# Attention and gated MLP on one core: in the first batch, the turn of u for column 1 is queued ahead of the score transposes, and the gating of a column is fixed ahead of the next squares on VectorE

## The chip, the cores and the metric

The kernel runs on one core of one Trainium2 chip. The metric is the device time of one execution in microseconds (us). The kernel before, run 11 times on one chip, gave 1217.6 to 1223.4 us.

Every ratio below is the record's ratio of a kernel's fast runs to those of the kernel before in the same rounds; it is not quite the ratio of the medians that stand beside it, nor exactly that of the plain means (u1_early: 1.0014 by means, 1.0008 on record). A 95% interval follows in brackets.

## The reference

Eight batches of attention with squared-ReLU scores and a gate `u`, then an MLP with a cosine activation over all 24064 tokens. It is cut to what matters:

```python
# u, v: [8, 3008, 256]   z: [8, 3008, 64]
scores = (1.0 / S) * np.matmul(z, z.transpose(0, 2, 1))
attn = np.maximum(scores, 0.0) ** 2
x = u * np.matmul(attn, v)              # the gating
h = x @ w_in                            # 256 -> 2048
out = (h * np.cos(h)) @ w_out           # 2048 -> 256
```

## The kernel before

A batch is worked off in six columns `c` of 512 tokens. For each block of scores, TensorE (PE) makes the scores, ScalarE (ACT) or VectorE (DVE) takes the ReLU, and DVE squares the result into a slot `s`. There are 18 slots for all score blocks. The output of a column is gated by `u`, which must stand transposed in SBUF. Two kinds of transposes are issued by SyncE (SP), in one fixed order: the turn of u (`ut<-ust`, 256 KB) and the score transposes (`s<-s`, 512 KB each), which spare PE the other half of the symmetric scores.

```python
def load(dst, src):                      # loads are issued by GpSimd, in order
    hold(nc.gpsimd.dma_start(dst, src))  # hold: wait until PE has come this far

def turn_u(b, c):
    ut = utpool.tile([P, NDH, CW], FP16, name="ut")
    hold(nc.sync.dma_start_transpose(... ut ..., ... ust[c % 2] ...))   # two ust buffers
    uts[(b, c)] = ut
...
def s_squares(b, c, R, p, banks):        # cut
    t = slot("a", b, c, R)
    ...
    nc.vector.tensor_tensor(             # writes the slot: it must wait for whoever still reads it
        t.rearrange("p s k w -> p s k w")[:, 2 * p:2 * p + 2], rv, rv, ALU.mult)
    if p == 1 and R > c and not direct(b, R, c):
        tt = slot("t", b, c, R)          # a second slot
        nc.sync.dma_start_transpose(... tt ..., ... t ...)
...
def finish(b, c):                        # the gating of a column
    for nh in range(NDH):
        for x, o, n in parts:
            nc.vector.tensor_tensor(
                x[:, nh, :], acc[nh][:, o:o + n], ut[:, nh, o:o + n], ALU.mult)
...
# the order of work, shortened; t counts steps, 8 (U) to a column
first = [load_v(0, 0), load_u(0, 0), load_v(0, 1), load_v(0, 2), load_u(0, 1)]
at(2, 0, lambda: load_u(0, 2))
for q in range(4):
    at(4 + 2 * q, 0, lambda q=q: load_w_in(q))
    at(17 + 2.5 * q, 0, lambda q=q: load_w_out(q))
at(t - 3.5 * U, 0, lambda b=b: load_z(b))             # z of the next batch
at(t + (c - 1.25) * U, 0, lambda b=b, c=c: load_u(b, c))
at(t + c * U + (1 if b or c not in (1, 2) else -3 * c), 0, lambda b=b, c=c: turn_u(b, c))
```

Column 3 is the first that uses the turned scores. Its first sums on DVE (`a_sums1`) read the first, fourth and seventh score transpose.

## Time and profile before

Time: 1220.31 us median of 4 runs (1218.51 to 1222.17) in the comparison with the changed kernel. The profiled run has a span of 1216.4 us.

From the page of the kernel before (busy time, share of the span, instructions; PEld is PE's loading of weights, POOL is GpSimd):

```profile
PE 1205.9 (99%) x8439; PEld 767.9 (63%) x8439; DVE 1028.0 (85%) x2073; ACT 833.1 (68%) x1744; POOL 146.0 (12%) x201
```

PE is full, so a microsecond counts only where PE is idle or its clock is low. The windows view (length of a stretch; busy time and number of instructions of PE, PEld, DVE, ACT and POOL; then granted clock, DMA share, GB/s) finds such stretches only before about 76 us:

```profile
36.00:44.00 8.00, 5.81 (x26) 1.81 (x24) 5.80 (x11) 3.27 (x7) 1.49 (x2) 0.86 1.13 170
44.00:52.00 8.00, 8.00 (x40) 3.01 (x39) 7.40 (x20) 5.27 (x11) 3.13 (x4) 0.93 1.41 176
52.00:60.00 8.00, 7.77 (x38) 2.95 (x38) 7.80 (x15) 6.30 (x13) 4.49 (x7) 1.00 1.70 193
...
76.00:84.00 8.00, 8.00 (x54) 4.80 (x54) 5.95 (x12) 3.60 (x8) 2.60 (x4) 1.00 0.88 130
```

The largest hole in PE's work is that of 38.9 to 41.1 us. In the timeline the number in brackets is the idle time before the instruction and what ended it:

```profile
40.34 1.29 DVE L382 TENSOR_TENSOR x<-acc,ut 128x512 f16<-128x512 f32 x2 [2.03 <-DMA ut<-ust]
40.81 1.49 POOL L121 DMA_DIRECT2D ust<-in_u_dram  x2 [11.59 <-DMA ut<-ust]
...
41.08 1.27 PE L353 MATMUL acc<-s,v 128*128 128x512 f16 x4 [2.19 <-DVE x L382]
```

DVE's gating waits for the turn of u, and PE waits for DVE. GpSimd, which issues all loads in order, also stands still for 11.59 us, since it can't refill the u buffer before it is turned.

The SP queue in the timeline:

```profile
12.87 1.36 SPq L181 DMA_TRANSPOSE ut<-ust  x1
16.26 15.91 SPq L310 DMA_TRANSPOSE s<-s  x3
32.34 3.35 SPq L181 DMA_TRANSPOSE ut<-ust  x1
35.78 4.21 SPq L310 DMA_TRANSPOSE s<-s  x1
40.16 1.23 SPq L181 DMA_TRANSPOSE ut<-ust  x1
41.48 28.67 SPq L310 DMA_TRANSPOSE s<-s  x7
```

The turn of u for column 1 is the third line. It stands behind three score transposes and lands at 40.2 us. The chain of waits (start, length, what) then shows the seventh score transpose in front of column 3:

```profile
32.34 7.91 DMA ut<-ust
...
48.46 11.76 DMA s<-s
60.25 0.42 DVE s L423
```

### The profile page before, as it was taken

The page shows a single profiled execution, that of the slowest core. Times are in us where ns is not written, and L with a number is a line of the kernel's source. Part 1 is how long each engine was busy: PE and PEld are TensorE (multiplying, and loading weights), DVE is VectorE, ACT ScalarE, POOL GpSimd, SP SyncE. Part 2 cuts the span into 40 slices and gives each one's busy share as a digit, 9 for nine tenths or more (in the row PEclk, how much of TensorE's full clock was granted, in tenths as well). Part 3 has the DMA queues.
Part 4 walks back from the last instruction along what each step waited for, and adds up shares of the span by engine and source line. Part 5 has one row for each costly group of instructions (what it writes and reads, how often), then busy time and mean ns, then how long its engine had stood idle before and what let it go on. Part 6 is the DMA issues. An engine that isn't in the chain of part 4 may idle for free.

```text
span 1216.4 us, 23077 instructions
## 1 busy us (share of the span) xinstructions
PE 1205.9 (99%) x8439; PEld 767.9 (63%) x8439; DVE 1028.0 (85%) x2073; ACT 833.1 (68%) x1744; POOL 146.0 (12%) x201
## 2 busy tenths in 40 slices
PE   8999999999999999999999999999999999999998
PEld 3356666666666666666666666666666666666666
DVE  8888988889888898888888888888888888888875
ACT  6667766677666776767767677676776767767555
POOL 4210111001010010100101001010110111100000
PEclk9999999999999999999999999999999999999999
DMA  9997957779686796767958579585795857957311
GB/s 162 178 161 118 143 97 121 123 121 149 96 116 124 124 146 105 119 111 121 152 105 123 102 120 155 102 133 101 111 160 97 132 104 109 162 94 120 74 31 48
DMA packets 484225, 145.02 MB, mean 119 GB/s; under 512 B 432400, under 2 KB 484112, under 8 KB 484112
## 3 DMA queue, kind: packets, MB, share of 16 engines
q1 hardware_dynamic: 356448, 88.73, 43.9%
q0 software_dynamic: 100400, 29.77, 24.4%
q10 hardware_dynamic: 27264, 25.06, 6.5%
q8 instruction: 66, 1.08, 0.4%
q14 instruction: 47, 0.39, 0.1%
HBM read 60.29 MB, written 24.64 MB: 70 GB/s over the span
## 4 chain that ended last, share of the span: by engine, by line
PE 96%; DMA 2%; DVE 1%; issue 0%; ACT 0%; DVEq 0%; ACTq 0%
PE w L517 27%; PE w L500 26%; PE acc L466 19%; PE acc L353 17%; PE w L265 6%; DMA s<-s 1%; PE acc L330 1%; DMA ut<-ust 1%; DMA v<-in_v_dram 1%; DVE s L303 0%; DVE g L507 0%; PE w L696 0%; DVE x L382 0%; DVE s L435 0%; ACT rt L301 0%
## 5 line engine op out<-in xcount | busy, mean ns | idle before, releaser
L504 ACT ACTIVATE c<-w 128x512 f16<-128x512 f32 x752 | 437.7, 621 | 259.3 <-PE w L500 206.5
L507 DVE TENSOR_TENSOR g<-w,c 128x512 f16<-128x512 f32 x752 | 492.3, 683 | 60.2 <-ACT c L504 57.4
L517 PE MATMUL w<-w_out,g 128*128 128x256 f16 x3008 | 448.8, 273 | 0.0
L500 PE MATMUL w<-x,w_in 128*128 128x512 f16 x1504 | 446.0, 379 | 0.0
L517 PEld LDWEIGHTS <-g 128*128 128x128 f16 x3008 | 294.0, 98 | 191.3
L353 PE MATMUL acc<-s,v 128*128 128x512 f16 (+1 forms) x1000 | 287.1, 380 | 2.4 <-DVE x L382 2.2
L301 ACT ACTIVATE rt<-w 128x512 f16<-128x512 f32 x489 | 253.2, 616 | 46.8 <-PE w L265 46.8
L303 DVE TENSOR_TENSOR s<-rt 128x1024 f16<-128x1024 f16 x254 | 172.7, 688 | 85.4 <-ACT rt L301 84.4
L500 PEld LDWEIGHTS <-w_in 128*128 128x128 f16 x1504 | 146.8, 98 | 73.8 <-issue 3.6
L466 PE MATMUL acc<-s,vsum 128*128 128x256 f16 (+1 forms) x1208 | 157.9, 270 | 0.9 <-DVE q L482 0.7
L121 POOL DMA_DIRECT2D ust<-in_u_dram x112 | 81.2, 731 | 570.5 <-PE acc L353 541.2
L353 PEld LDWEIGHTS <-v 128*128 128x128 f16 x1000 | 93.1, 98 | 77.1 <-issue 32.7
L466 PEld LDWEIGHTS <-vsum 128*128 128x128 f16 x1208 | 117.2, 98 | 20.0 <-issue 4.4
L466 PE MATMUL acc<-s,v 128*128 128x256 f16 (+1 forms) x906 | 117.6, 270 | 0.0
L466 PEld LDWEIGHTS <-v 128*128 128x128 f16 x906 | 85.3, 98 | 20.4 <-issue 12.4
L435 DVE TENSOR_TENSOR s<-s,s 128x1024 f16<-128x1024 f16 (+1 forms) x151 | 94.7, 668 | 2.7 <-PE acc L466 2.7
L265 PE MATMUL w<-zT 64*128 64x512 f16 (+3 forms) x684 | 91.0, 361 | 2.9 <-ACT zT L226 1.1
L524 ACT ACTIVATE ob<-w 128x256 f32<-128x256 f32 x188 | 71.2, 379 | 10.6 <-PE w L517 10.6
L382 DVE TENSOR_TENSOR x<-acc,ut 128x64 f16<-128x64 f32 (+7 forms) x178 | 68.6, 429 | 2.1 <-DMA ut<-ust 2.0
L282 ACT ACTIVATE rt<-w 128x512 f16<-128x512 f32 (+3 forms) x176 | 62.8, 451 | 10.5 <-PE w L265 10.5
L121 POOL DMA_DIRECT2D v<-in_v_dram x40 | 31.3, 788 | 298.3 <-PE acc L466 144.1
L425 DVE TENSOR_TENSOR s<-s 128x512 f16<-128x512 f16 (+1 forms) x151 | 61.2, 411 | 2.0
(37 smaller groups left out, 363.0 us busy)
## 6 DMA issues: line engine op xcount, KB each, us to landing
out_dram<-ob ACTq DMA_DIRECT2D x92, 256.0 KB, 2.2
ust<-in_u_dram POOLq DMA_DIRECT2D x80, 128.0 KB, 4.7
v<-in_v_dram POOLq DMA_DIRECT2D x16, 512.0 KB, 6.5
s<-s SPq DMA_TRANSPOSE x249, 4.4
v<-in_v_dram POOLq DMA_DIRECT2D x8, 448.0 KB, 9.1
zst<-in_z_dram POOLq DMA_DIRECT2D x14, 128.0 KB, 5.3
ust<-in_u_dram POOLq DMA_DIRECT2D x16, 96.0 KB, 5.0
w_in<-in_moe_w_in_dram POOLq DMA_DIRECT2D x4, 256.0 KB, 10.9
```

The source lines that it names most:

```text
L121: hold(nc.gpsimd.dma_start(dst, src))
L265: chain(nc.tensor.matmul(sp[:, s0 * P:], zt[h, R * K + k + 1 - lo, :], zt[h, j0 + s0:j0 + K, :].rearrange("p j w -> p (j w)"), start=True, ...
L301: nc.scalar.activation(rt[:, i, :], banks[k], AF.Relu)
L303: nc.vector.tensor_tensor(t.rearrange("p s k w -> p k s w")[:, 2 * p:2 * p + 2], rv, rv, ALU.mult)
L353: chain(nc.tensor.matmul(acc[:, 0:wn], vs(b, j // G)[:, j % G, nh * P:(nh + 1) * P], a, start=(start and n == 0), stop=(last and n == len( ...
L435: after(nc.vector.tensor_tensor(dst, src, sub, ALU.subtract).ins, before[-1], NOSYNC)
L466: chain(nc.tensor.matmul(acc[bank][:, cols], lhs[:, k, :], rhs[:, k, :] if old else rhs[:, :, k * P:(k + 1) * P], start=(n in (1, 5) and i ...
L500: chain(nc.tensor.matmul(hp, w_in16[:, k, ft * P:(ft + 1) * P], x[:, k, :], start=(k == 0), stop=(k == NDH - 1)))
L504: nc.scalar.activation(c16, hp, AF.Sin, bias=math.pi / 2.0, scale=inv_s2)
L507: nc.vector.tensor_tensor(gs[(m, ft // FG)][:, ft % FG, :], hp, c16, ALU.mult)
L517: chain(nc.tensor.matmul(ys[m][:, 0:D], gs[(m, f4)][:, ft % FG, ts * P:(ts + 1) * P], w_out16[:, ft, :], start=(ft == 0), stop=(ft == NFT ...
L524: nc.scalar.activation(obs[m][:, i, :], ys[m][:, 0:D], AF.Copy, bias=0.0, scale=inv_s2)
```

## The change

The intent is to close the hole at 38.9 us: the turn of u for column 1 is to be queued ahead of the score transposes, and DVE is to do the gating before it takes up the next squares.

```diff
-                nc.vector.tensor_scalar_max(rt[:, i, :], banks[k], 0.0)
+                behind(nc.vector.tensor_scalar_max(rt[:, i, :], banks[k], 0.0).ins)
...
-        nc.vector.tensor_tensor(
-            t.rearrange("p s k w -> p s k w")[:, 2 * p:2 * p + 2], rv, rv, ALU.mult)
+        ins = nc.vector.tensor_tensor(
+            t.rearrange("p s k w -> p s k w")[:, 2 * p:2 * p + 2], rv, rv, ALU.mult).ins
+        if direct(b, c, R):
+            behind(ins)
...   (in finish)
+        if direct(b, c, c):
+            ended[:] = [ins]
+
+    ended = []
+
+    def behind(ins):
+
+        if ended:
+            after(ins, ended[0], NOSYNC)
...
-            at(t + c * U + (1 if b or c not in (1, 2) else -3 * c), 0, lambda b=b, c=c: turn_u(b, c))
+            at(t + c * U + (1 if b or c > 2 else (0.7, -7.2, -6.0)[c]), 0, lambda b=b, c=c: turn_u(b, c))
```

A comparison of the instruction orders of the two builds shows that nothing moves on PE, DVE, ACT and GpSimd. On SP, the turn of u for column 1 goes from behind three score transposes to ahead of them.

More of the change, by code (lines that the diff above doesn't have):

```diff
@@ L302, in s_squares @@
         rv = rt.rearrange("p k (s w) -> p k s w", s=K)
-        nc.vector.tensor_tensor(
-            t.rearrange("p s k w -> p k s w")[:, 2 * p:2 * p + 2], rv, rv, ALU.mult)
+        ins = nc.vector.tensor_tensor(
+            t.rearrange("p s k w -> p k s w")[:, 2 * p:2 * p + 2], rv, rv, ALU.mult).ins
+        if direct(b, c, R):
+            behind(ins)
         if p == 1:
@@ L381, in finish @@
             for x, o, n in parts:
-                nc.vector.tensor_tensor(
-                    x[:, nh, :], acc[nh][:, o:o + n], ut[:, nh, o:o + n], ALU.mult)
+                ins = nc.vector.tensor_tensor(
+                    x[:, nh, :], acc[nh][:, o:o + n], ut[:, nh, o:o + n], ALU.mult).ins
+        if direct(b, c, c):
[4 more added lines that the diff above has]
+            after(ins, ended[0], NOSYNC)
     def v_sums(b, R):
```

## The prediction

> **What bounds it now.** The page has PE busy 1205.9 of 1216.4 us (99%); the windows view shows PE full from about 73 us on, so only how much earlier PE gets there counts. Before that there is one large hole: PE idle 2.19 us (38.9 to 41.08) until the gating of column 1 on DVE (x<-acc,ut), itself held 2.03 us by the turn of u (ut<-ust). That was issued at 32.34, behind three score transposes on the SP queue (from 16.26), and took 7.91 us. After the hole the granted clock is 0.5 for 42 to 44 and 0.72 for 44 to 46: about 1.6 us more. In all 3.8 us of PE.
>
> **What the change does.** Comparing instruction orders: PE, DVE, ACT and POOL are the same in both kernels. Fixing the gating moves nothing; it already stood there. The only difference is on the SP queue: the turn of u for column 1 goes ahead of three score transposes.
>
> **Costs.** The turn now waits for u of column 1 (issued at 9.46 and 10.54, landed 8.8 and 9.2 us later, at 19.7; I estimate 18.5 without competing transposes). It should land near 22 us, so the hole and its clock drop go: up to 3.8 us of PE, about 2.6 us of DVE idle (windows, 38 to 48).
>
> **How much is on the critical path.** Little. From 46 to 79 us DVE is nearly full, and the score transposes hold it: the chain shows a transpose s<-s from 48.46 to 60.22, ahead of a first sum (a_sums1) on DVE that waited 0.44 us for it. Its source was ready before 38.3: the queue makes it late. The SP queue is busy from 16.26 to 71.5. The Trainium skill, "DMA: Bandwidth & Descriptors", section "Issuing engines are not separate DMA queues", says that all issues share 16 engines; the packets agree: transposes move about 285 GB/s alone, some 30 GB/s while weights load (25 to 32 us). Turning u first gives the same bytes in another order, so that transpose should still land near 60 us (estimate 59 to 62: score transposes start about 3.5 us later, the turn's slot later is saved, and loads released by PE come some 3 us earlier and compete). DVE would arrive near 57.2 and wait about 3 us; PE idles near 58 to 61. The stall mostly moves. That idle may bring a second clock drop: "TensorE: Matmul & The Clock Gate", "Part 1: The HAM clock gate", ties the clock to recent activity; this trace drops after 2.2 us of idling.
>
> **Prediction.** 1220.8 us, 8 in 10 between 1218.0 and 1223.4. Faster by over 2%: 0.01; within 2%: 0.98; slower: 0.01.
>
> **What would show it.** Right: ut<-ust for column 1 lands near 22; no PE idle or clock drop at 38 to 46; a DVE wait of 2 to 3 us on a DMA s<-s ending near 60; PE idle of 1 to 3 us near 58 to 61; PE steady from about 73 as before. Wrong: that sum starts near 57, DVE has no DMA wait over 1 us, PE is full from about 70; then the gain is 2.5 to 3.8 us (about 1218).
>
> **What would make it wrong.** The transposes profit from the new order and the queue runs ahead; or earlier loads of z and w_out starve them, the sum waits to 62 and the kernel is 1 to 2 us slower.

## The result and the profile after

The changed kernel takes 1225.84 us median of 4 runs (1224.5 to 1226.6) against 1220.31; ratio 1.0044 [1.0023, 1.0065]. It is slower by about half a per cent. The profiled span is 1222.4 us, 6.0 us more than before. The second sums of column 3 on DVE (`s<-s,s`) start at 72.91 us instead of 66.92, also 6.0 us later: nothing after them adds to the loss.

The windows view of the changed kernel, the same stretches:

```profile
36.00:44.00 8.00, 7.92 (x42) 2.87 (x41) 6.04 (x12) 5.74 (x11) 2.12 (x3) 1.00 1.59 141
44.00:52.00 8.00, 6.54 (x30) 2.23 (x29) 6.17 (x15) 3.85 (x7) 4.60 (x6) 1.00 1.41 161
52.00:60.00 8.00, 3.02 (x8) 0.79 (x8) 4.22 (x8) 3.01 (x7) 0.00 (x0) 0.77 1.64 199
60.00:68.00 8.00, 7.65 (x30) 2.76 (x29) 6.37 (x13) 4.24 (x9) 2.29 (x3) 0.80 1.03 154
```

The hole at 38.9 us and its clock drop are gone, as intended. In their place PE is busy for only 3.02 of 8 us from 52 to 60, and the clock is low for longer. From 36 to 84 us PE is idle for 8.01 us (4.13 before), and the low clock costs 8 × 0.23 + 8 × 0.20 = 3.4 us (8 × 0.14 + 8 × 0.07 = 1.7 before). Together that is 5.6 of the 6.0 us.

The SP queue after:

```profile
11.83 9.62 SPq L181 DMA_TRANSPOSE ut<-ust  x2
21.56 27.38 SPq L312 DMA_TRANSPOSE s<-s  x4
49.11 1.25 SPq L181 DMA_TRANSPOSE ut<-ust  x1
50.45 26.64 SPq L312 DMA_TRANSPOSE s<-s  x7
```

The turn waits for u of column 1, which landed at 20.16 us, and is issued at 20.22. The first score transpose is issued at 21.56 instead of 16.26, which is 5.3 us late, but it lands 15.0 us late (38.18 instead of 23.23), beside the loads of w_in, which land between 34.5 and 40.9 us. The second lands 16.4 us late, the fourth 12.7 (54.7 instead of 42.05), the sixth 7.9. Most of the lateness arises at the head of the queue; later the queue makes up a part of it, but not in time.

What waits for them, from the timeline of the changed kernel:

```profile
44.50 0.69 DVE L303 TENSOR_TENSOR s<-rt 128x1024 f16<-128x1024 f16 x1 [2.28 <-DMA s<-s]
...
54.80 0.69 DVE L303 TENSOR_TENSOR s<-rt 128x1024 f16<-128x1024 f16 x1 [4.13 <-DMA s<-s]
...
56.95 0.58 PE L265 MATMUL w<-zT 64*128 64x512 f16 x1 [5.09 <-DVE g L518]
...
61.63 0.69 DVE L303 TENSOR_TENSOR s<-rt 128x1024 f16<-128x1024 f16 x1 [2.61 <-DMA s<-s]
```

These are squares (line L303), not first sums. They write slots that the second (landed at 44.41), the fourth (54.71) and the sixth (61.54) score transpose still had to read. DVE waits 9.0 us in all. ACT and PE fill the PSUM buffers behind it, and PE then stands for 5.09 us.

The loads, in GpSimd's timeline of the changed kernel:

```profile
35.88 1.49 POOL L121 DMA_DIRECT2D ust<-in_u_dram  x2 [6.63 <-PE acc L355]
41.32 0.74 POOL L121 DMA_DIRECT2D w_out<-in_moe_w_out_dram  x1 [3.95 <-PE w L265]
44.63 0.74 POOL L121 DMA_DIRECT2D w_out<-in_moe_w_out_dram  x1 [2.57 <-PE acc L355]
47.54 3.85 POOL L121 DMA_DIRECT2D zst<-in_z_dram  x5 [2.17 <-PE acc L332]
```

In the kernel before, the first of these came at 40.81 us, and the others followed:

```profile
44.50 0.74 POOL L121 DMA_DIRECT2D w_out<-in_moe_w_out_dram  x1 [2.21 <-PE w L265]
48.30 0.74 POOL L121 DMA_DIRECT2D w_out<-in_moe_w_out_dram  x1 [3.06 <-PE acc L353]
50.35 3.85 POOL L121 DMA_DIRECT2D zst<-in_z_dram  x5 [1.31 <-PE acc L330]
```

Now they come 2.8 to 4.9 us sooner, since neither the late turn nor the hole in PE holds them, and they meet a queue of transposes that is late.

### The profile page after: what moved, and what is told of

The parts are those of the page before. It is cut to its first block, busy times and chain, and to the rows that moved or that the text cites. A ratio compares the mean times of both kernels' runs of the same rounds, so it can differ in the third digit from the quotient of the medians.

```text
span 1222.4 us, 23078 instructions
## 1 busy us (share of the span) xinstructions
PE 1208.2 (99%) x8439; PEld 769.2 (63%) x8439; DVE 1028.4 (84%) x2073; ACT 833.4 (68%) x1744; POOL 146.0 (12%) x201
## 4 chain that ended last, share of the span: by engine, by line
PE 95%; DMA 3%; DVE 1%; ACT 0%; issue 0%; DVEq 0%
PE w L528 27%; PE w L511 26%; PE acc L477 19%; PE acc L355 17%; PE w L265 6%; DMA s<-s 3%; PE acc L332 1%; DVE g L518 0%; DVE s L303 0%; PE w L707 0%; ACT zT L226 0%; DVE s L446 0%; ACT rt L301 0%; DVE x L384 0%; DVE s L436 0%
## 5 line engine op out<-in xcount | busy, mean ns | idle before, releaser
L303 DVE TENSOR_TENSOR s<-rt 128x1024 f16<-128x1024 f16 x254 | 172.9, 688 | 93.6 <-ACT rt L301 83.7
L282 ACT ACTIVATE rt<-w 128x512 f16<-128x512 f32 (+3 forms) x176 | 62.8, 449 | 10.5 <-PE w L265 10.5
L436 DVE TENSOR_TENSOR s<-s 128x512 f16<-128x512 f16 (+1 forms) x151 | 61.4, 412 | 1.9
```

Source lines behind the costliest of these rows:

```text
L303: ins = nc.vector.tensor_tensor(t.rearrange("p s k w -> p k s w")[:, 2 * p:2 * p + 2], rv, rv, ALU.mult).ins
```

## The experiments

All kernels gave correct results. "Landing" is the moment at which a transfer's semaphore reaches its full count in the trace of the one profiled run. The table sums up all runs; the sixth score transpose is the one that stands out.

| kernel | median us | ratio to before [95%] | landing of the 2nd / 4th / 6th score transpose | profiled span |
|---|---|---|---|---|
| before | 1220.31 | 1 | 28.0 / 42.1 / 53.6 | 1216.4 |
| changed | 1225.84 | 1.0044 [1.0023, 1.0065] | 44.4 / 54.7 / 61.5 | 1222.4 |
| turn_only | 1226.49 | 1.0062 [1.0047, 1.0077] | 46.2 / 56.8 / 62.2 | 1223.3 |
| pins_only | 1219.19 | 0.9992 [0.998, 1.0004] | 27.7 / 42.7 / 56.5 | 1217.4 |
| wait_only | 1222.16 | 1.0013 [0.9992, 1.0033] | 32.8 / 41.0 / 52.8 | 1215.6 |
| behind_t1 | 1224.89 | 1.0033 [1.0011, 1.0056] | 36.0 / 46.7 / 59.3 | 1223.8 |
| behind_t2 | 1218.49 | 0.9992 [0.9966, 1.0019] | 27.2 / 42.2 / 53.6 | 1215.1 |
| u1_early | 1223.39 | 1.0008 [0.9983, 1.0033] | 33.6 / 46.2 / 59.6 | 1222.8 |
| w_in_late | 1226.18 | 1.0046 [1.0022, 1.0071] | 30.5 / 44.9 / 59.2 | 1223.7 |
| w_in_early | 1217.40 | 0.9979 [0.9954, 1.0003] | 35.1 / 40.5 / 52.8 | 1213.7 |
| more_slots | 1228.64 | 1.0063 [1.0041, 1.0084] | 44.7 / 56.2 / 67.7 | 1227.2 |
| loads_late | 1216.94 | 0.9978 [0.9947, 1.0008] | 35.9 / 44.5 / 51.6 | 1214.8 |
| after_loads_late | 1218.87 | 0.9989 [0.9971, 1.0007] | 40.8 / 48.2 / 54.8 | 1218.4 |
| after_w_in_early | 1216.34 | 0.9971 [0.9952, 0.9989] | 34.7 / 41.5 / 52.9 | 1214.1 |
| best1 | 1216.56 | 0.9976 [0.9956, 0.9995] | 36.4 / 41.8 / 58.3 | 1221.1 |
| best2 | 1216.79 | 0.9992 [0.9963, 1.0021] | 27.4 / 40.3 / 52.9 | 1213.8 |
| after_u3_late | 1228.17 | 1.0066 [1.0055, 1.0078] | 42.4 / 52.4 / 61.8 | 1226.0 |
| after_wz_late | 1221.42 | 1.0011 [0.9993, 1.0028] | 42.5 / 51.8 / 57.1 | 1219.2 |

In the profiled runs of all kernels but before and pins_only, where a hole in PE near 40 us is left (2.19 and 1.18 us), a sixth landing by 54.8 us goes with a span of 1218.4 us or less, and one at 57.1 us or later with 1219.2 us or more.

### The two halves of the change

`turn_only` takes `behind` out of the changed kernel; `pins_only` keeps it and puts the old place of the turn back.

```diff
 # turn_only, against the changed kernel
-            after(ins, ended[0], NOSYNC)
+            pass
 # pins_only, against the changed kernel
-(1 if b or c > 2 else (0.7, -7.2, -6.0)[c])
+(1 if b or c not in (1, 2) else -3 * c)
```

> The moved turn without the fixing of the gating: every engine's order and waits are those of the changed kernel. Fixing does nothing: 1224 to 1227 us, ratio near 1.004, sixth score transpose landing at 58 us or later in the profile. Fixing costs: near 1220 us.

> The fixing of the gating without the moved turn: every engine's order and waits are those of the kernel before. Fixing does nothing: within 0.2% of before, 1219 to 1222 us, sixth score transpose near 53 us.

turn_only: 1226.49 us; pins_only: 1219.19 us. Fixing the gating does nothing, alone or with the turn. The moved turn is the whole loss: turn_only shows it in rounds of its own (1.0062), and in the traces its order of work on every engine and on the SP queue is that of the changed kernel.

### First theory: the queue waits in order for a late load

Theory A was that SP stands until u of column 1 lands, so that the transposes lose a stretch without loads (20 to 25 us). Rival B was that the turn's own bytes and its place cost, wait or no wait.

`wait_only` keeps the order of the kernel before, and only makes the first score transpose wait for that load. `behind_t1` and `behind_t2` put the turn behind one or two score transposes, where its data has landed. `u1_early` loads u of column 1 sooner.

```diff
 # wait_only, against the kernel before
+                if (b, c, R) == (0, 0, K - 1):
+                    for ld in u1_loads:
+                        after(d.ins, ld, SYNC)
 # behind_t1: place -6.5 and, in turn_u, ...
+        if (b, c) == (0, 1):
+            after(d.ins, first_turns[0], NOSYNC)   # the first score transpose
 # behind_t2, against the changed kernel
-(0.7, -7.2, -6.0)[c]
+(0.7, -3.5, -6.0)[c]
 # u1_early, against the changed kernel
-load_v(0, 0), load_u(0, 0), load_v(0, 1), load_v(0, 2), load_u(0, 1)
+load_v(0, 0), load_u(0, 0), load_u(0, 1), load_v(0, 1), load_v(0, 2)
```

> The kernel before with its order kept (turn of u for column 1 behind three score transposes); only the first score transpose must also wait until u of column 1 has landed. Theory A (the in-order wait for the late load costs the transposes their free window before the weight loads start): first score transpose issued near 20 instead of 16.3 us, the second lands at 35 us or later instead of 28, DVE waits several us on DMA s<-s, and the turn of u is later still, so 1224 to 1230 us. Rival B (what costs is the turn's own 256 KB and its place ahead of the score transposes, not the waiting): within 1 us of before.

> The changed kernel with the turn of u for column 1 behind the first score transpose (still ahead of two). It then meets data that has landed (21.3 against about 20 us), so the queue does not stand still. Theory A: no loss against before; the hole at 38 to 41 us is gone, score transposes as in before up to about 1 us; 1217 to 1221 us. Rival B: two thirds of the loss stays, about 1223 to 1224 us.

> The changed kernel with the turn of u for column 1 behind two score transposes (ahead of one). Theory A: like behind_t1, 1217 to 1221 us, as no wait is in the queue; the turn is issued near 23.5 us and lands well before 38 us. Rival B: a third of the loss stays, about 1222 us.

> The changed kernel with its order of turns kept; u of column 1 is loaded before the second and third group of v instead of after. Then the turn ahead of the score transposes finds its data (landing near 14 instead of 20 us). Theory A: the loss goes, first score transpose issued by about 17 us, 1217 to 1221 us. Rival B: the turn is still ahead of all, 1225 to 1226 us as the changed kernel.

behind_t2 did what A asked for, but A fell with the others. With the wait alone, wait_only took 1222.16 us, below the 1224 to 1230 that A asked for and unclear against before. It is a weak test: in its profiled run the first score transpose was issued at 18.7 us, 2.5 us late where the changed kernel was 5.3, and that run was the fastest of its six. behind_t1 has no wait in the queue and yet took 1224.89 us, and u1_early, whose turn was issued at 13.6 us without waiting, still had a sixth landing at 59.6 us in its profile. B asked for about 1223 to 1224, 1222 and 1225 to 1226 us in the last three kernels; measured were 1224.89, 1218.49 and 1223.39. B has the direction for behind_t1 and is off for the others. The runs of one kernel spread widely here: behind_t2 from 1215.9 to 1225.4 us, u1_early from 1217.0 to 1224.9 us.

### Second theories: which loads lie beside the transposes

Theory A2 kept the lost stretch at 20 to 25 us, but named the loads of w_in that follow as the enemy. Rival D named the later loads, which PE releases sooner once its hole is gone.

```diff
 # w_in_late, against the changed kernel
-at(4 + 2 * q, 0, lambda q=q: load_w_in(q))
+at(10 + q, 0, lambda q=q: load_w_in(q))
 # w_in_early, against the kernel before
-at(4 + 2 * q, 0, lambda q=q: load_w_in(q))
+at(1 + 0.25 * q, 0, lambda q=q: load_w_in(q))
 # more_slots, against the changed kernel
-NSLOT = 18
+NSLOT = 20
 # loads_late, against behind_t1: w_out, z and u of columns 3 and 4 two steps later
-at(17 + 2.5 * q, 0, lambda q=q: load_w_out(q))
+at(19 + 2.5 * q, 0, lambda q=q: load_w_out(q))
-at(t - 3.5 * U, 0, lambda b=b: load_z(b))
+at(t - 3.5 * U + (2 if b == 1 else 0), 0, lambda b=b: load_z(b))
-at(t + (c - 1.25) * U, 0, lambda b=b, c=c: load_u(b, c))
+at(t + (c - 1.25) * U + (2 if b == 0 and c < 5 else 0), 0, lambda b=b, c=c: load_u(b, c))
```

> The changed kernel, its order of turns kept; only the four loads of w_in are released later (near 28 to 33 us instead of 22 to 28.5). New theory A2 (score transposes pushed out of the load-free stretch at 20 to 25 us run beside the loads of w_in, and the two together move some 120 GB/s where transposes alone move 285 and loads alone 185, so everything behind them is late): the first two score transposes land by about 28 us, DVE waits under 2 us on DMA s<-s, and the loss goes: 1216 to 1220 us. Rival B (the turn's place ahead of the score transposes costs by itself): 1225 to 1226 us, as the changed kernel. Rival D (the loss comes from later loads, of u for column 3, w_out and z, that PE releases earlier when its hole is gone): also about 1225 us.

> The kernel before, its order of turns kept; only the loads of w_in are released early (near 12 us, behind u of column 1), so that they fill the load-free stretch at 20 to 25 us. A2: the first two score transposes land at 30 us or later and the kernel loses, 1223 to 1228 us, though no turn has moved. Rivals B and D: within 1 us of before, about 1220 us.

> The changed kernel with 20 instead of 18 score slots, so that fewer squares on DVE must wait until a score transpose has read their slot. If late transposes cost through these slots: DVE's waits on DMA s<-s before the squares shrink from 9.0 us to under 6 us and the time falls to 1221 to 1224 us, while the transposes land as late as in the changed kernel. If the slots don't matter: 1225 to 1226 us.

> behind_t1 with the loads that PE releases after 35 us (u of columns 3 and 4, w_out, z) released two steps later, near where they came in the kernel before its hole was gone. Rival D: the 6.2 us wait of DVE on a score transpose (landing at 59.3 us) goes to under 2 us, 1217 to 1220 us. A2 alone: the second score transpose still lands at 36 us and the fourth at 46 us or later; the wait shrinks little, 1222 to 1225 us.

A2 fell twice. In w_in_late the first two transposes landed at 28.9 and 30.5 us, as hoped, and the loss stayed (1226.18 us): w_in had only been moved beside the third to fifth transposes (it landed between 33.7 and 42.7 us). In w_in_early the stretch at 20 to 25 us is filled with loads, the second transpose landed as late as 35.1 us, and the kernel was not slower but, at 1217.4 us, at least as fast as before. A late second transpose alone therefore makes no loss, and an early one does not prevent it. (In the changed kernel it landed later still, at 44.4 us, and DVE waited 2.28 us for it.)

loads_late supports D: holding back the later loads takes behind_t1 from 1224.89 to 1216.94 us, and in its profiled run DVE no longer waits for any score transpose.

more_slots missed. With 20 slots the assignment of all slots changes, so that DVE waits for the third and fifth transpose (3.7 and 3.0 us) and longer before the first sums (4.6 us). It was slower, 1228.64 us. It doesn't tell what the slots cost.

### Third theory: the lateness of the queue at 53 us

Theory E joins the two: loads and transposes side by side are slow, whatever loads they are. What counts is whether the fourth and sixth score transposes have landed when DVE wants their slots.

```diff
 # after_loads_late: the changed kernel with the three edits of loads_late
 # after_w_in_early: the changed kernel with the edit of w_in_early
 # best1: w_in_early, z and u as in loads_late, w_out at 17.5 + 2.5 * q
 # best2: behind_t2,  z and u as in loads_late, w_out at 17.5 + 2.5 * q
```

> The changed kernel, turn of u first; only the loads that PE releases after 35 us (u of columns 3 and 4, w_out, z) are released two steps later. Theory E (the loss is the queue's lateness by about 53 us, where DVE must write into slots that the fourth and sixth score transposes still read; loads beside transposes make it late, and the early turn lets those loads come 4 us sooner): the sixth transpose lands before 56 us instead of 61.5, DVE waits under 4 us on DMA s<-s before the squares (9.0 in the changed kernel), 1217 to 1221 us. If the loss is settled before 35 us (turn ahead of the transposes, w_in): the fourth still lands at 54 us or later, 1224 to 1227 us.

> The changed kernel, turn of u first; only the loads of w_in are released near 12 us as in w_in_early. E: fewer loads are left beside the transposes after 28 us, the sixth lands before 56 us, 1216 to 1220 us. If the turn's place costs by itself: still 1223 us or more.

> The kernel before with w_in released early (as in w_in_early) and u of columns 3 and 4, w_out and z released a half to two steps later: an attempt at a version that beats both. E: no DVE wait on DMA s<-s over 1 us, 1214 to 1217 us. If late releases only move the waits (PE waiting for w_out): 1217 to 1220 us.

> behind_t2 (turn of u behind two score transposes) with u of columns 3 and 4, w_out and z released a half to two steps later. E: the runs near 1222 to 1225 us that behind_t2 had become rare, median 1215 to 1217 us.

E held where it was tested against the place of the turn. Both kernels keep the turn first, exactly as the changed kernel does. after_loads_late came to 1218.87 us and after_w_in_early to 1216.34 us, instead of 1225.84. The sixth transpose landed at 54.8 and 52.9 us. DVE's waits before squares and first sums, from 36 us on in after_w_in_early, are down to:

```profile
DVE s L303 <- DMA s<-s: 0.3, 1, 0.3
DVE s L434 <- DMA s<-s: 0.3, 1, 0.3
```

The windows of 12 to 16 and 25.2 to 36 us show the rate (last number, GB/s). First the kernel before, then the changed kernel, then after_w_in_early:

```profile
12.00:16.00 4.00, 4.00 (x26) 1.53 (x24) 3.92 (x8) 3.01 (x6) 0.00 (x0) 1.00 1.45 197
25.20:36.00 10.80, 10.80 (x57) 3.56 (x55) 9.42 (x16) 7.47 (x16) 1.41 (x2) 1.00 1.33 150
39.00:42.00 3.00, 0.92 (x4) 0.42 (x4) 1.66 (x3) 1.28 (x3) 1.19 (x2) 0.95 1.25 265
```

```profile
25.20:36.00 10.80, 10.80 (x58) 3.57 (x55) 9.42 (x16) 7.47 (x16) 1.53 (x3) 1.00 1.36 123
```

```profile
25.20:36.00 10.80, 10.80 (x58) 3.67 (x56) 9.42 (x16) 7.62 (x15) 0.00 (x0) 1.00 1.45 186
```

From 12 to 16 us loads run alone in the kernel before, at 197 GB/s. From 39 to 42 us transposes run almost alone, at 265 GB/s. From 25.2 to 36 us, where transposes and the loads of w_in are in flight together, the sum falls below both: 150 GB/s before, 123 GB/s in the changed kernel, which has more of its transposes in that stretch. In after_w_in_early, whose w_in has landed by then, it is 186 GB/s. With other loads the sum need not fall so far. In the kernel before, from 48.3 to 62.8 us, transposes and loads of w_out, z and u are in flight throughout, and the sum, 190 GB/s, is near that of loads alone; in the changed kernel, with w_out and z from 44.6 to 58.4 us, it is 170. The line of the kernel before:

```profile
48.30:62.80 14.50, 13.70 (x67) 5.12 (x66) 14.06 (x31) 11.08 (x23) 6.88 (x9) 1.00 1.57 190
```

best1 and best2 aimed at a version that beats both. best1 did by its median (0.9976 [0.9956, 0.9995]), yet its profiled run was its longest, with a span of 1221.1 us, the sixth landing at 58.3 us and a wait of DVE of 4.8 us for it, where E had asked for none over 1 us. best2 is unclear: four runs at 1215.5 to 1216.9 us and two near 1224 to 1226, so the long runs that were expected to become rare are two of six, as in behind_t2. The best version is after_w_in_early, the changed kernel with w_in loaded early. It is 0.3% faster than the kernel before; since w_in_early alone has 0.9979 [0.9954, 1.0003], it is not shown that the moved turn has a part in this gain.

### Which later loads

> The changed kernel with only the load of u for column 3 held until about 40.5 us, as in the kernel before. If this load, no longer held by the late turn, is what costs: sixth score transpose before 56 us, 1217 to 1221 us. If it is w_out and z: still 1223 us or more.

> The changed kernel with only w_out and z (and u of column 4) released two steps later, u of column 3 as early as in the changed kernel. If w_out and z are what costs: sixth score transpose before 56 us, 1217 to 1221 us. If it is u of column 3: still 1223 us or more. If both share it: 1220 to 1224 us in this run and in after_u3_late.

```diff
 # after_u3_late, against the changed kernel
-at(t + (c - 1.25) * U, 0, lambda b=b, c=c: load_u(b, c))
+at(t + (c - 1.25) * U + (2.9 if b == 0 and c == 3 else 0), 0, lambda b=b, c=c: load_u(b, c))
 # after_wz_late: w_out and z as in loads_late, u of column 4 later by 2, u of column 3 not
```

u of column 3 is not what costs: with it held to 40.81 us the kernel took 1228.17 us. With w_out and z held (and u of column 4, which both kernels load only after 60 us), it took 1221.42 us, a ratio of 1.0011 against 1.0062 for turn_only, whose order of work is that of the changed kernel, in the same rounds. No branch of the expectation was met to the letter: the sixth transpose landed at 57.1 us, not before 56, and the time lies just above the 1221 asked for. But by that measure w_out and z, released too soon for a late queue, stand for most of the loss. What is left in that kernel are 4.2 us of waits of DVE on score transposes, the longest 3.2 us; it had been 9.0:

```profile
DVE s L303 <- DMA s<-s: 4.2, 2, 3.2
```

Early loads alone do not make the loss either: after_w_in_early issues w_out and z as early as the changed kernel (41.53, 44.84 and 46.90 us against 41.32, 44.63 and 47.54) and loses nothing. It takes both, a queue that is already late and loads that come soon.

## Why the prediction was wrong

- **The hole.** Right. The turn landed at 24.6 us (predicted near 22), and PE idle and clock drop at 38 to 46 us are gone. The estimate that the load would land at 18.5 us was off: it landed at 20.16.
- **What the change moves.** Right. Only the SP order moves, and pins_only (0.9992) shows that fixing the gating does nothing.
- **"Turning u first gives the same bytes in another order, so that transpose should still land near 60 us (estimate 59 to 62".** This is the step that failed. The bytes are the same but their rate is not: how fast they move depends on what is in flight beside them. The first transpose was issued 5.3 us late and landed 15.0 us late, the fourth landed 12.7 us late, the sixth 7.9 us and the seventh 4.5 us late (64.7 instead of 60.2). The Trainium skill's statement that all issues share 16 engines ("DMA: Bandwidth & Descriptors", section "Issuing engines are not separate DMA queues"), which the prediction used, is in line with the trace: from 25.2 to 36 us of the kernel before, the transposes moved 0.36 MB beside the loads of w_in, some 33 GB/s, against 265 almost alone. It doesn't say that sharing costs throughput, and the prediction took the sharing as free. The traces' 123 and 150 GB/s beside w_in, against 197 for loads alone and 265 for transposes almost alone, show that it was not free there.
- **Where DVE would wait.** Missed. The prediction looked only at data flow, at the first sum that reads the seventh transpose. The waits came earlier, at squares that must not overwrite a slot still being read: 2.28, 4.13 and 2.61 us.
- **"PE idles near 58 to 61" and a second clock drop.** The mechanism was right, the size and place were not: 5.09 us from 51.86 to 56.95, and a half clock for 6.8 us in the trace's record of the clock. The prediction let this stall replace the closed hole, with no net loss (1220.8 us).
- **"earlier loads of z and w_out starve them" with 1 to 2 us slower.** This was named as the way to be wrong, and it is what loads_late, after_loads_late and after_wz_late show. The size was 5.5 us, not 1 to 2.

The late turn had held back PE by its hole, and so the loads that PE releases. That cost 3.8 us of PE time, and it kept w_out and z away from the score transposes 2.8 to 3.7 us longer.

Open is why transposes and the loads of w_in together move less than either alone (123 to 150 GB/s), and transposes with w_out, z and u more (170 to 190), which these runs measure but don't explain. Open is also what makes single runs of one kernel differ by up to 10.6 us (loads_late): the landings are known for one profiled run of each kernel only. And more_slots could not show how much a looser assignment of slots would save.

## What to carry to other kernels

When a DMA is moved ahead in an in-order queue, don't only ask whether its own wait goes away: list every instruction that waits for the transfers behind it, also those that only want to overwrite what these read. A stall that is removed also removes a brake: find out what the stalled engine releases (here loads), and give those a later or an earlier place of their own. Loads and on-chip transposes in flight together moved less than transposes alone (123 to 190 GB/s against 265), and beside w_in less than loads alone, so put big loads where nothing yet waits for the transposes beside them (here at 12 to 28 us: in w_in_early the second score transpose then landed only at 35.1 us, and DVE did not wait for it).

## What the Trainium skill lacked or had wrong

- "DMA: Bandwidth & Descriptors", section "Issuing engines are not separate DMA queues", says that DMAs of all issuing engines interleave on the same 16 DMA engines. It lacks what SBUF to SBUF transposes and loads in flight together move in sum: here 197 GB/s for loads alone, 265 GB/s for mostly transposes, 123 to 150 GB/s for transposes with the loads of w_in, 170 to 190 GB/s with those of w_out, z and u.
- The same page, section "Rules for kernel authors", says of silent corruption that "A transpose next to ordinary DMAs needs nothing". No run here speaks against that, as all kernels gave correct results; what the page lacks is that such a neighbour can cost speed: a score transpose landed 16.6 us after its issue (the first, in the changed kernel) beside the loads of w_in, and 4.3 us after its issue where the last load landed 1.1 us after it was issued (the sixth, at 57.27 us).
- "TensorE: Matmul & The Clock Gate", Part 1, gives at least one idle window of about 3.4 us before the clock falls to half. Here 2.19 us of idling were enough (kernel before, 38.9 to 41.1 us); the half clock then lasted 3.4 us, and 6.8 us after the 5.09 us of the changed kernel. These lengths agree with one and two windows of the page. The length of a single hole did not decide alone: 1.38 us were followed by a drop in after_loads_late (60.0 to 61.4 us), 1.70 us by none in loads_late (72.8 to 74.5 us).
